# Normalised linear attention and a gated channel mix: full-width attention algebra, blends as scale and add, and a new planner for the order of instructions

## The chip, the cores and the metric

The kernel runs on one core of one Trainium2 chip (trn2). Times are device microseconds (us), the median of several executions. PE is the matmul engine (TensorE), PEld its weight loads, DVE the vector engine, ACT the scalar engine, POOL and SP the two that mostly issue DMA here. Some executions fall into a slow state (here 278 to 314 us, with a lower granted PE clock).

## The reference

```python
kv  = einsum('bhsd,bhse->bhde', k, v)          # batch 8, heads 8, seq 576, head 64
out = einsum('bhsd,bhde->bhse', q, kv)
x   = out / sqrt(mean(out*out, -1) + 1e-6) * g_norm   # then heads side by side: [8, 576, 512]
xk  = mu_k * x + (1 - mu_k) * x_prev           # x_prev: x of the token before
xr  = mu_r * x + (1 - mu_r) * x_prev
y   = sigmoid(xr @ w_r) * (relu(xk @ w_k)**2 @ w_v)   # 512 -> 1024 -> 512
```

Matmul operands are bf16. The channel mix goes in 9 groups of 512 tokens; the attention in 8 batches of 576. Group g needs batches up to g (group 8 up to 7), so attention for later batches runs between the mix's matmuls.

## The kernel before

Pieces of work are handed to a planner in Python, which simulates the engines and so fixes the order in which each engine's instructions are emitted; each engine then runs its list in order. The parts that matter:

```python
# statistics and normalisation, once per batch (all four pairs of heads, 32 rows each)
nc.tensor.matmul(get(pst)[32*hp:32*hp+32, half, 0:HS], sel2, sq.t[:, hp, ...])       # L360 sums of squares
nc.scalar.preload_act_table_set("natural_log_exp_and_others")                       # L365
nc.scalar.activation(out=get(ln)[rows], in_=pst.t[rows, :, 0:HS], func=AF.Ln, bias=eps[rows], scale=1.0/HD)
nc.scalar.activation(out=get(rs)[rows], in_=ln.t[rows], func=AF.Exp, scale=-0.5)    # rs = 1/rms
nc.tensor.matmul(get(ps)[:, i, 0:HS], selg[rows], rs.t[rows, half, :])              # L384 spread rs*g to 128 rows
nc.vector.tensor_mul(out=xT.t[...], in0=get(uT)[...], in1=ps.t[...])                # L391 product, one operand in PSUM
# ... d = xT - xT of the token before ...
nc.vector.scalar_tensor_tensor(out=dst[:, hp, ...], in0=d.t[:, hp, :],              # L413 fused blend
    scalar=mu_sb[:, m+hp:m+hp+1], in1=xT.t[:, hp, 0:S], op0=ALU.mult, op1=ALU.add)
```

The matmuls of the mix are L453 (w_k), L476 (w_r) and L495 (w_v); L480 is the sigmoid, L457 the ReLU. Attention's PSUM tiles, called `at`, have two buffers; the mix's, `mm`, have two as well.

## Time and profile before

| | before |
|---|---|
| time, median of fast runs | 240.4 us |
| PE, DVE, ACT busy | 87%, 67%, 52% of the span |
| first w_r matmul; first w_k matmul of group 0, group 1 | 23.7; 32.4, 60.8 us |
| table loads of ACT | 17, 1.28 us each |

The page's first lines, busy us with the share of the span:

```profile
span 238.5 us, 3893 instructions
PE 207.4 (87%) x1586; PEld 98.0 (41%) x1586; DVE 158.7 (67%) x263; ACT 123.3 (52%) x154; POOL 25.1 (11%) x39
```

PE is the busiest, and its necessary work is easily counted. The timeline of PE late in the run (start us, length us, engine, line, operation, operands, shape, count) shows the mix alone:

```profile
179.83 7.07 PE L453 MATMUL mm<-xk,w_k 128*128 128x512 bf16 x32
186.74 3.62 PE L476 MATMUL mm<-w_r,xr 128*128 128x512 bf16 x16
```

From 179.83 to 186.74 us are 32 matmuls, 216 ns each; 9 groups of 80 make 155 us. The rest of the span is attention, waits, the start and the end. The largest wait is between groups 0 and 1 (same view; in brackets the idle time before, and what ended it):

```profile
52.84 0.29 PE L384 MATMUL at<-rs,selg 32*128 32x288 bf16 x2
...
54.64 0.30 PE L384 MATMUL at<-rs,selg 32*128 32x288 bf16 x2 [0.71 <-DVE xT L391]
55.30 0.30 PE L384 MATMUL at<-rs,selg 32*128 32x288 bf16 x2 [0.37 <-DVE xT L391]
...
60.83 1.05 PE L453 MATMUL mm<-xk,w_k 128*128 128x512 bf16 x2
```

For 8 us no mix matmul runs: PE feeds small matmuls to DVE, which makes the product L391 from PSUM, then the blends. After it DVE is the limit for a while. The view of stretches (stretch, its length, then busy us of each engine, granted clock, DMA share, GB/s):

```profile
60.00:100.00 40.00, 37.57 (x329) 16.75 (x327) 39.22 (x65) 27.09 (x36) 4.62 (x6) 0.97 0.81 135
```

DVE is busy for 39.22 of 40 us, ACT for 27. And the groups of instructions of ACT and DVE that the change touches (line, engine, operation, operands, shapes, count, then busy us, mean ns of one, idle time before them):

```profile
L413 DVE SCALAR_TENSOR_TENSOR xr<-d,mu_sb,xT 128x576 bf16<-128x576 bf16 x32 | 24.2, 813 | 0.0
L391 DVE TENSOR_TENSOR xT<-uT,at 128x576 bf16<-128x576 bf16 x29 | 20.8, 750 | 7.4 <-PE at L384 7.2
L365 ACT ACT_TABLE_LOAD x10 | 12.8, 1283 | 0.2
L366 ACT ACTIVATE ln<-at,eps 128x576 f32<-128x576 f32 x7 | 5.2, 741 | 0.1
```

### The profile page before, as it was taken

The numbers are of one execution on the slowest core, as the hardware profiler recorded it, in microseconds if no ns is written. First come the engines' busy times: TensorE is split into PE (matmuls) and PEld (weight loads), VectorE is DVE, ScalarE is ACT, GpSimd is POOL, SyncE is SP. The second block draws the span as 40 slices with busy tenths as digits, with TensorE's granted clock in tenths as the row PEclk, the third lists the DMA queues.
The fourth block names the chain that finished last, engine by engine and source line by source line (L and its number), as shares of the span: only waits on it lengthen the run. The fifth ranks groups of instructions, "written<-read, shape, count | busy, mean of one in ns | idle before, by whom it ended". The sixth has DMA issues, their size and how long they took to land.

```text
span 238.5 us, 3893 instructions
## 1 busy us (share of the span) xinstructions
PE 207.4 (87%) x1586; PEld 98.0 (41%) x1586; DVE 158.7 (67%) x263; ACT 123.3 (52%) x154; POOL 25.1 (11%) x39
## 2 busy tenths in 40 slices
PE   0573699896999989979799999998999999999971
PEld 0431146443534434443453378333444444444430
DVE  1278915659999999958975996799599324224231
ACT  2379147735678913964577449547713513604500
POOL 8860002300300300030000000000000000000000
PEclk9999999996799999999999999999999999999998
DMA  5999999999993595359530130024004114015033
GB/s 79 184 206 207 204 203 204 204 207 267 201 198 47 69 203 115 91 65 194 131 87 3 46 107 25 0 58 121 0 0 134 45 33 144 3 37 139 1 88 88
DMA packets 26817, 26.46 MB, mean 111 GB/s; under 512 B 1704, under 2 KB 21680, under 8 KB 26800
## 3 DMA queue, kind: packets, MB, share of 16 engines
q0 software_dynamic: 21008, 16.78, 45.8%
q1 hardware_dynamic: 5792, 9.45, 14.1%
q8 instruction: 12, 0.20, 0.3%
q14 instruction: 5, 0.04, 0.0%
HBM read 33.56 MB, written 9.44 MB: 180 GB/s over the span
## 4 chain that ended last, share of the span: by engine, by line
PE 64%; DVE 16%; ACT 10%; DMA 5%; issue 2%; POOL 0%; SPq 0%; DVEq 0%; ACTq 0%; POOLq 0%
PE mm L495 22%; PE mm L453 22%; PE mm L476 11%; DVE out L499 4%; DMA q<-in_q_dram 3%; DVE xT L391 3%; PE at L315 2%; DMA out_dram<-out 2%; PE at L293 2%; ACT L365 2%; DVE xr L413 2%; DVE xk L413 2%; DVE sq L344 2%; ACT relu L457 2%; PE at L335 1%
## 5 line engine op out<-in xcount | busy, mean ns | idle before, releaser
L495 PE MATMUL mm<-w_v,sqk 128*128 128x512 bf16 x288 | 68.2, 380 | 1.7 <-DVE out L499 1.7
L453 PE MATMUL mm<-xk,w_k 128*128 128x512 bf16 (+1 forms) x320 | 67.6, 361 | 1.4 <-DVE out L499 1.4
L457 ACT ACTIVATE relu<-mm 128x1024 bf16<-128x1024 f32 x36 | 36.3, 1020 | 48.1 <-PE mm L453 48.1
L453 PEld LDWEIGHTS <-w_k 128*128 128x128 bf16 x320 | 30.3, 98 | 31.0 <-issue 3.2
L495 PEld LDWEIGHTS <-sqk 128*128 128x128 bf16 x288 | 25.7, 98 | 33.3 <-issue 4.1
L499 DVE TENSOR_TENSOR out<-mm,sig 128x1024 f32<-128x1024 f32 (+1 forms) x20 | 22.3, 1115 | 24.2 <-PE mm L495 17.8
L476 PE MATMUL mm<-w_r,xr 128*128 128x512 bf16 x144 | 36.5, 402 | 2.1 <-DVE xr L413 1.6
L460 DVE TENSOR_TENSOR sqk<-relu 128x1024 bf16<-128x1024 bf16 x36 | 24.6, 689 | 18.2 <-ACT relu L457 18.0
L172 ACT CAST uT<-at 128x576 bf16<-128x576 f32 x26 | 16.0, 640 | 24.4 <-PE at L335 24.4
L391 DVE TENSOR_TENSOR xT<-uT,at 128x576 bf16<-128x576 bf16 (+1 forms) x31 | 21.7, 731 | 7.4 <-PE at L384 7.2
L480 ACT ACTIVATE sig<-mm 128x1024 bf16<-128x1024 f32 x18 | 18.5, 1027 | 12.0 <-PE mm L476 11.7
L413 DVE SCALAR_TENSOR_TENSOR xr<-d,mu_sb,xT 128x576 bf16<-128x576 bf16 x32 | 24.2, 813 | 0.0
L413 DVE SCALAR_TENSOR_TENSOR xk<-d,mu_sb,xT 128x576 bf16<-128x576 bf16 x32 | 24.1, 812 | 0.1
L476 PEld LDWEIGHTS <-xr 128*128 128x128 bf16 x144 | 14.3, 102 | 21.6 <-issue 4.2
L315 PE MATMUL at<-ident,q 96*128 96x96 bf16 x186 | 13.6, 221 | 1.4 <-DMA q<-in_q_dram 0.9
L315 PEld LDWEIGHTS <-q 96*128 96x128 bf16 x192 | 11.9, 107 | 6.3 <-issue 1.8
L172 ACT COPY qT<-at 128x576 bf16<-128x576 bf16 x19 | 11.8, 644 | 4.0 <-PE at L315 3.8
L344 DVE TENSOR_TENSOR sq<-uT 128x576 bf16<-128x576 bf16 x32 | 13.0, 453 | 0.4 <-ACT uT L172 0.3
L365 ACT ACT_TABLE_LOAD x10 | 12.8, 1283 | 0.2
L232 POOL DMA_DIRECT2D q<-in_q_dram x10 | 7.3, 735 | 51.4 <-PE at L315 41.0
L384 PE MATMUL at<-rs,selg 32*128 32x288 bf16 x60 | 8.9, 298 | 3.9 <-DVE kv L174 1.1
L407 DVE TENSOR_TENSOR d<-xT 128x2304 bf16<-128x2304 bf16 (+2 forms) x10 | 11.2, 1119 | 0.3
(47 smaller groups left out, 114.2 us busy)
## 6 DMA issues: line engine op xcount, KB each, us to landing
out_dram<-out SPq DMA_DIRECT2D x24, 192.0 KB
k<-in_k_dram POOLq DMA_DIRECT2D x7, 576.0 KB, 10.3
v<-in_v_dram POOLq DMA_DIRECT2D x7, 576.0 KB, 12.4
q<-in_q_dram POOLq DMA_DIRECT2D x7, 576.0 KB, 11.5
out_dram<-out SPq DMA_DIRECT2D x24, 128.0 KB
out_dram<-out SPq DMA_DIRECT2D x24, 64.0 KB
w_k<-in_moe_w_k_dram POOLq DMA_DIRECT2D x1, 1024.0 KB, 12.5
w_v<-in_moe_w_v_dram POOLq DMA_DIRECT2D x1, 1024.0 KB, 16.9
```

The source lines that it names most:

```text
L172: nc.scalar.copy(out=dst, in_=src)
L315: nc.tensor.transpose(t[:, e, NP * i:NP * i + NP], qin.t[:, 2 * hp + e, 128 * i:128 * i + 128], ident[:NP, :NP])
L344: e.tensor_tensor(out=get(sq)[:, hp, :], in0=flat(hp), in1=flat(hp), op=ALU.mult)
L391: nc.vector.tensor_mul(out=xT.t[:, hs, xs], in0=get(uT)[:, hs].rearrange("q h i jj p -> q h (i jj p)")[:, :, cs], in1=ps.t[:, 0:step, 0:HS])
L413: nc.vector.scalar_tensor_tensor(out=dst[:, hp, c0:c0 + S], in0=d.t[:, hp, :], scalar=mu_sb[:, m + hp:m + hp + 1], in1=xT.t[:, hp, 0:S], o ...
L453: nc.tensor.matmul(get(ps)[:, fc % 2, a0:a1], w_k_sb[:, cc, 128 * fc:128 * fc + 128], xk[:, cc, x0:x0 + a1 - a0], start=(cc == 0), stop=(c ...
L457: nc.scalar.activation(out=get(rt), in_=ps.t, func=AF.Relu)
L460: nc.vector.tensor_mul(out=get(sqk)[:, 2 * f2:2 * f2 + 2, :], in0=rt.t, in1=rt.t)
L476: nc.tensor.matmul(get(ps)[:, ci % 2, :], xr[:, cc, n0:n0 + 128], w_r_sb[:, cc, :], start=(cc == 0), stop=(cc == NHP - 1))
L480: nc.scalar.activation(out=get(sg), in_=ps.t, func=AF.Sigmoid)
L495: nc.tensor.matmul(get(ps)[:, ci % 2, :], sqk.t[:, fc, 128 * ci:128 * ci + 128], w_v_sb[:, fc, :], start=(fc == 0), stop=(fc == NFC - 1))
L499: nc.vector.tensor_mul(out=get(ot)[:, xs, :], in0=ps.t[:, xs, :], in1=sg.t[:, xs, :])
```

## The change

Its intent: full 128x128 matmuls in the attention (the kv of two heads on the diagonal of one block), the sums of squares by a block of ones so that they come out already spread over the 128 rows, the product then in SBUF, DVE's blends in faster forms, g multiplied into w_r and w_k, an early start by hardware-queue loads, and a planner with smaller latencies, stage targets and filler matmuls that keep PE's clock up at the start. The diff cut to its core:

```diff
-            nc.scalar.preload_act_table_set("natural_log_exp_and_others")        # was ahead of every Ln
-            nc.scalar.activation(out=get(ln)[rows], in_=pst.t[rows, :, 0:HS], func=AF.Ln, bias=eps[rows], ...)
-            nc.scalar.activation(out=get(rs)[rows], in_=ln.t[rows], func=AF.Exp, scale=-0.5)
+    add({"ACT": 1.3}, lambda _: nc.scalar.preload_act_table_set("natural_log_exp_and_others"), due=-1999, ...)  # once
+        for hp in range(NHP):                                                    # per pair of heads, all 128 rows
+            def ss_mm(...):   nc.tensor.matmul(get(ps)[:, i, 0:HS], ones, sq.t[:, hp, ...])
+            def ln_act(...):  nc.scalar.activation(out=get(ln), in_=ps.t[:, :, 0:HS], func=AF.Ln, bias=eps, scale=1.0/HD)
+            def exp_act(...): nc.scalar.activation(out=get(rs)[:, hp]..., in_=ln.t, func=AF.Exp, scale=-0.5)
+            a = add({"ACT": act_us(S, False, True)}, ln_act, ..., table="ln")    # the planner counts one set
+            exps[hp] = add({"ACT": act_us(S, True)}, exp_act, ..., table="ln")   # for both functions
-                nc.vector.tensor_mul(out=xT.t[:, hs, xs], in0=get(uT)[...], in1=ps.t[...])          # PSUM operand
+                nc.vector.tensor_mul(out=xT.t[:, hs, NP:NP+S], in0=uT.t[:, hs], in1=rs.t[:, hs])    # SBUF only
-            nc.vector.scalar_tensor_tensor(out=dst[...], in0=d.t[:, hp, :], scalar=mu_sb[...], in1=xT.t[...], ...)
+                    for hp in range(hp0, hp0 + n):
+                        nc.vector.tensor_scalar(out=get(md)[:, hp], in0=d.t[:, hp], scalar1=cols[...], op0=ALU.mult)
+                    nc.vector.tensor_tensor(out=dst[:, hs, ...], in0=md.t[:, hs], in1=xT.t[:, hs, 0:S], op=ALU.add)
+                nc.vector.tensor_scalar(out=dst, in0=dst, scalar1=cols[:, 8:9], ...)   # g into w_r (1x) and w_k (2x)
+            e.dma_start(out=first[n], in_=part(n, 0, 0, 2))     # first pair of heads, fp32, hardware queues; casts follow
+                nc.tensor.matmul(get(warm_ps)[:, 0, 0:128], zero[...], zero[...])      # filler in planned gaps at the start
... (transposes, kv blocks, planner latencies and stage targets cut)
```

## The prediction

> **What bounds it now.** Span 238.5 us, granted clock 0.98. PE is 87% busy and leads the chain of waits (PE 64%, DVE 16%, ACT 10%, DMA 5%). Its floor: the channel mix is 9 groups x 80 matmuls of 512 columns. From 173 us PE's timeline has 16 in 3.45 us, 216 ns each (the Trainium skill, "TensorE: Matmul & The Clock Gate", Wait — 56ns, not 53.3ns?, gives 215.7 ns warm; the trace agrees). So 155.4 us. Attention costs PE, per batch, from the chain: kv 0.88, transposes 4 x 0.26, u about 1.0, statistics 0.36, spreading 4 x 0.23: 4.2 us; seven batches inside the mix make 29.4. First w_r matmul 23.7 us, last w_v matmul ends 233.8: 210.1 - 155.4 - 29.4 = about 25 us lost between them, nearly all before 166 us:
> - 3.6 us at the start: matmuls wait for DVE's xr blends.
> - about 8 us at 52.7-60.8, between group 0 and group 1: group 1 needs batch 1 and DVE works through xT, d, xk. PE goes cold too (clock 0.65 to 0.78 in 54-66, about 3 us).
> - the rest at 66-166: DVE is 97-99% busy in 60-100 (busy by stretches).
>
> **The change, costed.**
> - Blends: 64 fused ones of 0.81 us (one element per cycle) become per batch 8 scales and two adds. The skill, "VectorE: DVE Perf Modes", the perf-mode tier table, has tensor_scalar at 4x and tensor_tensor at 2x in bf16. The trace agrees for the add (2304 columns in 1.36 us); no run yet shows the scale, estimate from the page 0.23 us. 6.5 -> about 4.5 us a batch.
> - xT product from PSUM, 4 x 0.75, becomes SBUF-only, about 1.3 us. kv copies 4 x 0.42 become 2 x 0.35.
> - Against it: ln and exp run on all 128 rows per head pair, 1.4 -> about 5.2 us of ACT a batch (4 x (0.67+0.62)).
> - PE: spreading goes (-0.92), the ones-block sums cost 8 x 0.12 instead of 0.36, the rest about equal: 4.2 -> 3.9 us a batch.
> DVE drops from about 16 to 13 us a group before copies, ACT rises from 10 to 13.5; both fit.
> - Start: first head pair by fp32 hardware-queue loads plus casts (first matmul 7.6 us now, then about 5), fewer table loads, w_r matmuls by head pair. First w_r matmul about 17.5.
> - Loads run near 205 GB/s until 57 us. Batch 1 is complete about 35 us now; with the earlier start about 34, in halves. Its last half still needs about 11 us of dependent work, so group 1 cannot start before about 44 (60.8 now); PE still loses about 5 us there.
>
> **Sum.** 17.5 + 155.4 + 7 x 3.9 + 6 (tail: last product, store) = 206; plus 5 at the batch 1 boundary, 3 to 4 for other stalls and cold clock: span about 215, time about 217 us (before: time minus span 2.7). Range 207 to 228. Faster 0.94, same 0.05, slower 0.01. The gain is idle PE time before 166 us.
>
> **What would show it.** First w_r matmul at 16-19 us; group 1's first w_k matmul at 41-48; scales near 0.23 us; DVE under 70% busy, ACT 70-75%; no stretch with DVE over 95%; last groups 17.3 us each; PE busy sum within 5 us of 207.
>
> **What would make it wrong.** ACT as the new limit: ln/exp and u copies holding the two "at" PSUM buffers; extra table loads; batch 1 later than its data allows; the 4x scales not at 4x.

## The result, and the profile after

The kernel after takes 250.2 us (four fast runs, 248.4 to 251.2), the kernel before 240.4 (three): slower by 4.0% (ratio 1.0402, interval 1.035 to 1.046). All ratios here are from fast runs alone; they are not quite the ratios of the medians that are quoted.

```profile
span 248.8 us, 4251 instructions
PE 212.2 (85%) x1730; PEld 111.1 (45%) x1730; DVE 152.8 (61%) x287; ACT 168.1 (68%) x198; POOL 28.2 (11%) x43
```

DVE fell a little; ACT rose by 45 us. ACT's groups, in the view that was shown of before:

```profile
L450 ACT ACTIVATE ln<-at,eps 128x576 f32<-128x576 f32 x32 | 22.4, 738 | 1.1 <-PE at L447 0.8
L453 ACT ACTIVATE rs<-ln 128x576 bf16<-128x576 f32 x32 | 20.5, 677 | 0.3
L450 ACT ACT_TABLE_LOAD x16 | 20.5, 1283 | 0.3
L453 ACT ACT_TABLE_LOAD x16 | 20.5, 1283 | 0.3
L578 ACT ACT_TABLE_LOAD x7 | 9.0, 1283 | 0.1
```

The Ln and Exp work itself grew as the prediction had it (43 us, 5.4 a batch). But there are 40 table loads, with the one at the very start, instead of 17: after batch 0 one at every switch from Ln to Exp and one at every switch back, so that each pair of loads serves one or two pairs of heads. ACT's timeline in batch 0, then in batch 1:

```profile
14.46 0.68 ACT L453 ACTIVATE rs<-ln 128x576 bf16<-128x576 f32 x1
15.04 0.72 ACT L450 ACTIVATE ln<-at,eps 128x576 f32<-128x576 f32 x1
...
39.63 1.28 ACT L450 ACT_TABLE_LOAD   x1
40.93 0.74 ACT L450 ACTIVATE ln<-at,eps 128x576 f32<-128x576 f32 x1
41.69 1.28 ACT L453 ACT_TABLE_LOAD   x1
42.98 0.68 ACT L453 ACTIVATE rs<-ln 128x576 bf16<-128x576 f32 x1
...
44.21 1.28 ACT L450 ACT_TABLE_LOAD   x1
```

In batch 0, after the one request by name, Ln and Exp alternate with no load at all. After the first sigmoid a load stands at every switch between the two. The planner believed that they share one (`table="ln"` on both). What that does to the other engines is in the waits (engine, line, for whom; us in total, times, longest):

```profile
DVE xT L468 <- ACT rs L453: 17.9, 14, 3.3
PE at L421 <- DVE qT L199: 6.4, 3, 2.2
PE at L374 <- ACT ln L450: 5.7, 2, 2.9
PE mm L601 <- ACT sig L578: 3.1, 1, 3.1
```

and in PE's timeline of group 3:

```profile
117.69 2.76 PE L548 MATMUL mm<-xk,w_k 128*128 128x512 bf16 x12
122.66 0.41 PE L421 MATMUL at<-qT,kvb 128*128 128x288 bf16 x2 [2.21 <-DVE qT L199]
```

The chain of waits tells how an Exp stops PE through DVE's queue: between the product and the copy of the next batch's q lie the copy of the token before, a copy of kv, d, the scales and the xr blend.

```profile
117.51 0.68 ACT rs L453
...
118.21 0.77 DVE xT L468
...
121.85 0.77 DVE qT L199
...
122.66 0.41 PE at L421 x2
```

The copy of q doesn't need that Exp. It stands behind the product in DVE's list, because the plan expected the Exp earlier.

A table of the first w_k matmul of each group, from PE's timelines, shows where time goes (two of the experiments below are listed already; "end" is the last matmul):

| us | g0 | g1 | g3 | g4 | g5 | g6 | g7 | g8 | end |
|---|---|---|---|---|---|---|---|---|---|
| before | 32.4 | 60.8 | 114.3 | 137.7 | 160.5 | 179.8 | 197.1 | 214.4 | 233.8 |
| after | 29.0 | 59.6 | 114.2 | 139.9 | 164.2 | 188.4 | 207.2 | 224.4 | 244.0 |
| one table set | 29.4 | 55.4 | 101.4 | 123.8 | 145.9 | 168.1 | 185.7 | 202.9 | 222.5 |
| longer warm-up | 28.4 | 54.5 | 99.7 | 122.1 | 144.2 | 166.3 | 184.0 | 201.2 | 220.7 |

The kernel after is never more than 3.4 us ahead, level at group 3, and then loses 2.3, 1.5 and 4.9 us in groups 3 to 5, as long as there is attention in the mix, and 1.5 us more in group 6. (Group 2 is left out, since the kernel before mixes its first matmuls with the end of group 1.) The prediction was 217 us, in a range of 207 to 228: wrong in sign.

### The profile page after: what moved, and what is told of

Read it like the earlier page. It is cut to its first block, busy times and chain, and to the rows that moved or that the text cites. A ratio compares the mean times of both kernels' runs of the same rounds, so it can differ in the third digit from the quotient of the medians.

```text
span 248.8 us, 4251 instructions
## 1 busy us (share of the span) xinstructions
PE 212.2 (85%) x1730; PEld 111.1 (45%) x1730; DVE 152.8 (61%) x287; ACT 168.1 (68%) x198; POOL 28.2 (11%) x43
## 4 chain that ended last, share of the span: by engine, by line
PE 45%; ACT 28%; DVE 15%; issue 5%; DMA 4%; SPq 1%; DVEq 0%; ACTq 0%
PE mm L548 18%; PE mm L601 11%; PE mm L574 8%; ACT L450 7%; ACT ln L450 7%; ACT rs L453 4%; ACT L453 3%; PE at L402 3%; ACT sig L578 2%; PE at L421 2%; DVE md L493 2%; DVE out L605 2%; DMA rows<-in_g_norm_dram 2%; DVE xr L496 2%; DVE qT L199 2%
## 5 line engine op out<-in xcount | busy, mean ns | idle before, releaser
L548 PE MATMUL mm<-xk,w_k 128*128 128x512 bf16 (+1 forms) x320 | 70.7, 367 | 3.6 <-DVE w_k L309 1.4
L468 DVE TENSOR_TENSOR xT<-uT,rs 128x1152 bf16<-128x1152 bf16 (+1 forms) x18 | 12.4, 690 | 17.9 <-ACT rs L453 17.9
L450 ACT ACTIVATE ln<-at,eps 128x576 f32<-128x576 f32 x32 | 22.4, 738 | 1.1 <-PE at L447 0.8
L578 ACT ACTIVATE sig<-mm 128x1024 bf16<-128x1024 f32 x18 | 18.2, 1024 | 7.0 <-PE mm L574 6.9
L493 DVE TENSOR_SCALAR md<-d,cols 128x576 bf16<-128x576 bf16 x64 | 21.2, 368 | 0.3
L453 ACT ACTIVATE rs<-ln 128x576 bf16<-128x576 f32 x32 | 20.5, 677 | 0.3
L453 ACT ACT_TABLE_LOAD x16 | 20.5, 1283 | 0.3
L450 ACT ACT_TABLE_LOAD x16 | 20.5, 1283 | 0.3
L421 PE MATMUL at<-qT,kvb 128*128 128x288 bf16 x64 | 13.8, 300 | 8.0 <-DVE qT L199 6.4
L277 POOL DMA_DIRECT2D k<-in_k_dram x11 | 8.1, 737 | 66.3 <-PE at L374 63.3
L435 DVE TENSOR_TENSOR sq<-uT 128x1152 bf16<-128x1152 bf16 (+1 forms) x20 | 12.6, 633 | 3.0 <-ACT uT L197 2.7
L199 DVE COPY qT<-at 128x1152 bf16<-128x1152 bf16 (+1 forms) x16 | 11.2, 700 | 3.7 <-PE at L402 3.6
L402 PE MATMUL at<-ident,q 96*64 96x96 bf16 x384 | 13.2, 223 | 0.0
```

The lines of the kernel that those rows point to most:

```text
L402: nc.tensor.transpose(t[64 * e:64 * e + 64, hp - hp0, NP * j:NP * j + NP], qin.t[:, 2 * hp + e, HD * j:HD * j + HD], ident[:NP, :NP])
L421: nc.tensor.matmul(get(ps)[:, i, 0:HS], kv[:, hp, :], qT.t[:, hp, HS * i:HS * i + HS], start=True, stop=True)
L450: nc.scalar.activation(out=get(ln), in_=ps.t[:, :, 0:HS], func=AF.Ln, bias=eps, scale=1.0 / HD)
L453: nc.scalar.activation(out=get(rs)[:, hp].rearrange("q (i c) -> q i c", i=2), in_=ln.t, func=AF.Exp, scale=-0.5)
L493: nc.vector.tensor_scalar(out=get(md)[:, hp], in0=d.t[:, hp], scalar1=cols[:, m0 + hp:m0 + hp + 1], scalar2=None, op0=ALU.mult)
L548: nc.tensor.matmul(get(ps)[:, fc % 2, a0:a1], w_k_sb[:, cc, 128 * fc:128 * fc + 128], xk[:, cc, x0:x0 + a1 - a0], start=(cc == 0), stop=(c ...
```

## The experiments

Thirteen kernels ran. All results are correct but for the last, which is wrong.

**1. One table set for Ln and Exp, the same plan.** The planner's calls are untouched, so the order of all pieces is that of the kernel after; only the request comes back, and only where a sigmoid has come between.

```diff
             def ln_act(_, ps=ps, ln=ln):
+                if table_now[0] != "ln":
+                    nc.scalar.preload_act_table_set("natural_log_exp_and_others")
+                    table_now[0] = "ln"
                 nc.scalar.activation(out=get(ln), ...)
         def r_sig(_, ps, sg):
+            table_now[0] = "sig"
```

> The kernel after, same plan and same arithmetic; the joint ln-and-exp table set is asked for by name before the first Ln after a Sigmoid, so table loads fall from 40 to 14 (26 x 1.28 = 33 us of ACT). Theory T1 (the loads are the cause of the loss: PE waits for ACT's ln and exp, which wait for loads): 212 to 222 us, ACT busy about 135 us, the gaps of PE behind ACT ln gone. Rival T2 (the ln and exp work on all 128 rows, 43 us instead of 14, holds the PSUM buffers whatever the loads do): 240 us or more. Rival T3 (the plan's order on in-order engines is at fault, above all DVE's queue between qT copies and blends): 230 to 245 us, with gaps of 2 us per group left in front of the u matmuls.

Measured: 228.3 us, ratio 0.948 (0.943 to 0.953). From the two ratios, 26 loads fewer (33 us of ACT) are worth (1.040 - 0.948) x 240.4 = 22 us, and turn a loss of 4% into a gain of 5%. ACT is busy for 133.6 us, as T1 had it, but the time lies above T1's range and below those of its rivals; so T1 holds for 22 us and doesn't explain the whole distance to the prediction. T2 is out. In ACT's timeline of batch 1 the Exp follows its Ln in 0.03 us; in the kernel after it came at 42.98, although that one's Ln was 0.47 us earlier:

```profile
41.40 0.74 ACT L454 ACTIVATE ln<-at,eps 128x576 f32<-128x576 f32 x1
42.17 0.68 ACT L457 ACTIVATE rs<-ln 128x576 bf16<-128x576 f32 x1
```

The loads that are left are 14, of which these stand ahead of an Ln:

```profile
L452 ACT ACT_TABLE_LOAD x6 | 7.7, 1283 | 0.1
```

T3's sign, gaps of 2 us ahead of the u matmuls, is gone. PE's timeline at the place where the kernel after lost 2.21 us:

```profile
107.86 0.41 PE L422 MATMUL at<-qT,kvb 128*128 128x288 bf16 x2 [0.23 <-DVE qT L199]
```

In the waits, DVE's product waited 17.9 us for Exp in the kernel after, and now:

```profile
DVE xT L472 <- ACT rs L457: 1.7, 2, 1.1
```

In the view of stretches PE and DVE are the busier for it; the kernel after had 32.35 us of PE, 27.25 of DVE and 34.83 of ACT here:

```profile
60.00:100.00 40.00, 38.49 (x297) 19.80 (x300) 34.22 (x64) 32.34 (x43) 3.08 (x4) 1.00 0.79 133
```

**2. Ln twice, in the kernel with one table set.** Is it the load that hurts, or ACT's time in that place? The Ln is issued a second time with the same result.

```diff
                 nc.scalar.activation(out=get(ln), in_=ps.t[:, :, 0:HS], func=AF.Ln, ...)
+                nc.scalar.activation(out=get(ln), in_=ps.t[:, :, 0:HS], func=AF.Ln, ...)
```

> One table set, and every Ln issued twice with the same result: 32 x 0.74 = 24 us more of ACT in the same place of the chain sums - Ln - Exp, no table load added. T1 in the form that it is ACT time in that chain that costs, whoever spends it: 12 to 20 us slower than with one table set (240 to 248 us). If only the loads themselves hurt (a flush of the engine beyond their 1.28 us): under 6 us slower.

Measured: 239.2 us (three fast runs), ratio 0.989 (0.984 to 0.993); that is, by the ratios, 9.8 us more than with one table set for 24 us of ACT, 0.41 us per us, where the loads cost 22 / 33 = 0.66. It lies between the two forecasts, short of 12 and above the rival's 6 us: time of ACT between the sums and the product costs though no load is added. Why a load costs more per us than a second Ln was not tested.

**3. The kernel before without its request.** The old kernel has Ln and Exp once per batch.

```diff
         def st_act(_):
             rows = slice(32 * hp0, 32 * hp0 + 32 * n)
-            nc.scalar.preload_act_table_set("natural_log_exp_and_others")
```

> The kernel before without its request for the joint table set ahead of each Ln. Its Ln and Exp run once per batch on all head pairs, so loads only rise from 17 to 21, by one in each of seven batches, less three at the start: ACT busy +5 us. If the harm of the missing request depends on the split into head pairs (a load before nearly every Ln and Exp): within 2 us of before. If any two loads in that chain cost PE in full: 5 us or more slower.

Measured: 244.7 us, ratio 1.017 (1.011 to 1.024), between the two forecasts: 4.2 us for a net 4 loads (5 us of ACT). The net hides two effects, which the profile separates: with three loads fewer at the start group 0's first w_k matmul comes at 31.0 us instead of 32.4, and with one more between Ln and Exp in each of seven batches group 7's comes at 200.7 instead of 197.1. So the seven cost 1.4 + 3.6 = 5.0 us, 0.7 each, against 22 / 26 = 0.85 each in the kernel after. The first guess, that only the split into head pairs makes the missing request expensive, is wrong per load. The split multiplies their number: 7 more in the batches here, 26 there.

**4. The blends, each way.** First the kernel before with its fused blends as scale and add; then the kernel with one table set with fused blends.

```diff
-            nc.vector.scalar_tensor_tensor(out=dst[...], in0=d.t[:, hp, :], scalar=mu_sb[...], in1=xT.t[...], ...)
+            nc.vector.tensor_scalar(out=md[:, hp], in0=d.t[:, hp, :], scalar1=mu_sb[...], op0=ALU.mult)
+            nc.vector.tensor_tensor(out=dst[...], in0=md[:, hp], in1=xT.t[:, hp, 0:S], op=ALU.add)
```

> The kernel before with its 64 fused blends replaced by a scale and an add each, nothing else; the plan's order is kept. DVE pays 64 x (0.29 + 0.38) = 43 us instead of 48 us if ops run back to back as in the kernel after (measured there: 0.57 us for two scales, 0.76 us for an add of two head pairs). If the blend form matters at all in a DVE-bound stretch, 235 to 240 us; if it is too small to matter, 240 to 242 us.

Measured: 241.9 us, ratio 1.0074 (1.001 to 1.013): no gain, rather a little loss.

> The kernel after with one table set as in the other run, but with the fused blends of before (64 x 0.81 us) in place of scales and adds; same plan. If the blend form was a real gain of the change: 3 to 10 us slower than the run with one table set. If DVE has slack once the loads are gone: within 2 us of it.

Measured: 228.3 us, ratio 0.950 (0.945 to 0.956), the same as with scale and add. The form of the blends, which the prediction counted as 2 us of DVE a batch, is worth nothing measurable either way (both runs kept a plan made for the other form). A scale of 576 columns takes 0.37 us alone and two in a row 0.57 (in the chain of waits, from the end of the operation before); the add of two head pairs takes 0.76. DVE's busy time in all is 155.2 us with fused blends and 151.5 with one table set: 3.7 us, or 0.5 a batch. In the old kernel, where each add is of one head pair, the split saves nothing: 159.4 us against 158.7.

**5. The new planner alone.** The kernel before, its pieces and durations unchanged, put in order by the new planner class, without fillers.

```diff
-class Piece: ...            # the planner of before
-class Planner: ...
+class Piece: ...            # that of after: smaller latencies, 0.25 us of slack for PE
+class Planner: ...
-    plan.run()
+    plan.run(lambda p: 0.25)
```

> The kernel before in every operation, but put in order by the new planner class (its latencies, its 0.25 us of slack for PE; no filler matmuls). The kernel with one table set is 12 us under before. If that gain is the planner's latencies: 228 to 233 us. If it is the new arithmetic and stage targets (SBUF product, pairs of head pairs, start): 238 to 245 us.

Measured: 242.5 us, ratio 1.0037 (1.001 to 1.007). The planner's class as such brings nothing; stage targets could not be tried apart from the pieces that they belong to.

**6. The product at its old speed.** In the kernel with one table set, rs is kept in fp32, so that the SBUF product runs at the rate that it had from PSUM; the planner doesn't know.

```diff
-        "rs": (1, (128, NHP, S), BF16),
+        "rs": (1, (128, NHP, S), FP32),
```

> One table set, with rs in fp32, so that the product uT x rs runs at the rate that it had from PSUM before (0.75 us per head pair instead of 0.38): 1.5 us more of DVE per batch, all else as with one table set. If the relief of DVE by the SBUF product is a good part of the 12 us that the kernel with one table set wins over before: 3 us or more slower (ratio above 0.96). If DVE has slack: under 1.5 us (0.948 to 0.955).

Measured: 237.4 us, ratio 0.988 (0.984 to 0.991): 9.5 us lost, of the 12.5 that the kernel with one table set wins over before. In the view of groups the product of two head pairs takes 1350 ns, against 758 in the kernel after (first line):

```profile
L468 DVE TENSOR_TENSOR xT<-uT,rs 128x1152 bf16<-128x1152 bf16 x14 | 10.6, 758 | 17.3 <-ACT rs L453 17.3
L472 DVE TENSOR_TENSOR xT<-uT,rs 128x1152 bf16<-128x1152 bf16 x14 | 18.9, 1350 | 1.1 <-ACT rs L457 1.1
```

Only 8 x 1.2 = 9.6 us of DVE were added, and nearly all of it reaches the end. The plan was fixed for the fast product here, so this is the price of a slow product in this plan; in a plan made for it the price may be less. In experiment 4, 3.7 us more of DVE in the same plan cost nothing that was measured. Whether that is the place in DVE's queue or the smaller amount was not tested.

**7. The start: g out of DVE's queue.** With the loads gone, 11 us to the predicted time are left. Group 0's first w_k matmul comes at 29.4 us where the prediction had about 21. It waits for DVE, whose last ops there scale w_k by g. Three runs take that away. The first lets ACT scale w_k:

```diff
-                            T0 + 1 + 4 * i, f"g.w_k{i}", {"DVE": both["DVE"]}))
+                            T0 + 1 + 4 * i, f"g.w_k{i}", {"ACT": both["ACT"]}))
```

> One table set as in the first run, and the scaling of w_k by g (two ops of 0.8 us on DVE, last in DVE's queue before group 0's first w_k matmul at 29.5 us) moved to ACT, which stands idle there. If the start is held by DVE's queue: first w_k matmul near 28 us and about 1 to 2 us faster than with one table set alone (226 to 227.5 us). If the start is held by something else (the data, the hidden-layer chain of the last head pair): within 0.5 us.

Measured: 230.5 us (three fast runs), ratio 0.954 (0.951 to 0.957), slower than with one table set if anything. The planner drew up another plan for it: inconclusive. The second gives up the scaling and adds ln g in the Exp (g is |noise| + 0.5 in the reference's inputs, so positive; a kernel for any g could not do this):

```diff
-                nc.scalar.activation(out=get(rs)[:, hp]..., in_=ln.t, func=AF.Exp, scale=-0.5)
+                nc.scalar.activation(out=get(rs)[:, hp]..., in_=ln.t, func=AF.Exp, bias=lng, scale=-0.5)
-    p_wr = scale_w(w_r_sb, load_w(...), ...)       # and the two of w_k
+    p_wr = load_w(...)
```

> One table set, and g is no longer multiplied into w_r and w_k (three DVE ops, 2.4 us, all before group 0's first w_k matmul); Exp adds ln g as a bias instead, a few hundredths of a us per Exp. If folding g into the weights held up the start: first w_r matmul about 1 us earlier, first w_k matmul 2 to 3 us earlier, 225 to 227 us in all. If not: within 0.7 us of the run with one table set, or slower by the dearer Exp.

Measured: 230.9 us, ratio 0.957 (0.953 to 0.961). The start came as expected (first w_r at 18.2, first w_k at 28.0, group 1 at 53.1 us, 2.3 us ahead of one table set), but the new plan let group 1 last from 53.1 to 82.9 us, 5 us longer than with one table set. Again two things changed. So the third keeps the plan: the scaling pieces stay in it with their times, and emit nothing.

```diff
         def fn(eng):
-            if eng == "ACT":
-                nc.scalar.mul(out=dst, in_=dst, mul=cols[:, 8:9])
-            else:
-                nc.vector.tensor_scalar(out=dst, in0=dst, scalar1=cols[:, 8:9], scalar2=None, op0=ALU.mult)
+            pass
```

> The earlier run without weight scaling also made the planner draw up another plan, which lost 4 us in group 1; here the plan is that of the run with one table set (the scaling pieces stay in the plan and emit nothing), and ln g is Exp's bias. If DVE's queue holds up the start: first w_k matmul near 28 us against 29.4, and 0.5 to 1 per cent faster than with one table set (ratio to before 0.938 to 0.945). If the start's lateness doesn't reach the end: ratio 0.946 to 0.952.

Measured: 228.0 us, ratio 0.948 (0.944 to 0.953): no gain, and the first w_k matmul at 29.8 us. And with batch 0's xk scales made by ACT on top:

```diff
+                        if fine and m0 == 0:
+                            nc.scalar.mul(out=get(md)[:, hp], in_=d.t[:, hp], mul=cols[:, m0 + hp:m0 + hp + 1])
+                            continue
                         nc.vector.tensor_scalar(out=get(md)[:, hp], in0=d.t[:, hp], ...)
```

> As the run before it, and batch 0's four scales for xk are made by ACT, idle there, instead of DVE (4 x 0.29 us off DVE's queue at 24 to 28 us). If DVE's queue bounds the start: first w_k matmul another 0.5 to 1.1 us earlier and the ratio to before another 0.3 per cent lower. If not: no change.

Measured: 228.5 us, ratio 0.951 (0.947 to 0.954), no change. Taken alone, these two say that work behind the xr blends is not what holds the start. But there is a second thing in the stretches of the run with the plan kept (granted clock is the third number from the right):

```profile
24.00:26.00 2.00, 0.60 (x2) 0.11 (x2) 1.86 (x6) 0.01 (x1) 0.00 (x0) 1.00 1.28 203
26.00:28.00 2.00, 1.99 (x6) 0.76 (x7) 1.90 (x6) 1.02 (x1) 1.06 (x2) 0.64 1.31 201
28.00:30.00 2.00, 2.00 (x6) 0.76 (x5) 1.15 (x3) 0.01 (x1) 0.58 (x1) 0.50 1.32 205
```

PE did little from 20 to 26 us, and when the matmuls came its clock went to half. The run with the xk scales on ACT has it too (0.50 from 24 to 30 us), so its "no change" does not clear DVE's queue either.

**8. A longer warm-up.** The fillers go on until batch 0's last xr blend, 13 more of them; else as in the run with the plan kept.

```diff
-    p_warm = add({"PE": 0.0}, lambda _: None, deps=[last_exp[0]], bufs=[warm_ps], ...)
+    p_warm = add({"PE": 0.0}, lambda _: None, deps=[x_ready[0]["r"][-1]], bufs=[warm_ps], ...)
```

> As the run with folding out and the plan kept, with the filler matmuls carried on until batch 0's last xr blend: 13 more fillers in the two gaps between the w_r matmuls at 20 to 26 us, nothing else. In the run without them the last ten w_r matmuls took 3.94 us (2.33 in the kernel after), so the gain of the shorter DVE queue was eaten by a slower PE. If the clock ate it: those ten take 2.2 to 2.4 us, first w_k matmul near 28.2 instead of 29.75, ratio to before 0.936 to 0.944. If the clock drops for another reason or the start doesn't matter: 0.946 to 0.951.

Measured: 226.9 us, ratio 0.944 (0.940 to 0.947), the best correct kernel; its six runs (226.5 to 227.3) all lie under the four without the fillers (227.5 to 228.7, same chip). First w_k at 28.4 us, the ten matmuls in 2.33 us. The stretch that had a clock of 0.64 (same view):

```profile
26.00:28.00 2.00, 1.81 (x9) 0.86 (x10) 1.93 (x6) 1.02 (x1) 0.94 (x2) 1.00 1.31 200
```

So in these profiles the half clock had eaten the shorter queue. Not every profile without the added fillers shows it: the kernel after, one table set and fused blends had their ten in 2.33 us too; experiment 6 and the last three kernels of experiment 7 took 3.75 to 4.45.

**9. Work ahead of the xr blends taken away**. Batch 0's four subtractions are left out; the result is wrong.

```diff
             def diff(_, hs=slice(hp0, hp0 + n)):
+                if fine:
+                    return
-   in0=d.t[:, hp], scalar1=cols[...]
+   in0=xT.t[:, hp, NP:NP + S] if fine else d.t[:, hp], scalar1=cols[...]
```

> As the run with the longer warm-up, but batch 0's four subtractions are left out and its scales read xT instead (a wrong result on purpose): 4 x 0.4 us off DVE ahead of the xr blends. If DVE feeds the start: last xr blend 1 to 1.6 us earlier, first w_k matmul near 27 instead of 28.4, and the total lower by about as much (ratio to before 0.936 to 0.940 against 0.9436). If the data or ACT's last Exp sets it: last xr blend at most 0.5 us earlier and the total within 0.5 us.

Measured: 226.0 us, ratio 0.939 (0.936 to 0.942), against 0.944 with them. DVE's last xr blend of batch 0, with the subtractions and then without:

```profile
25.68 0.46 DVE L499 TENSOR_TENSOR xr<-md,xT 128x576 bf16<-128x576 bf16 x1
```

```profile
24.61 0.46 DVE L501 TENSOR_TENSOR xr<-md,xT 128x576 bf16<-128x576 bf16 x1
```

It is 1.07 us earlier, the first w_k matmul 1.1 us (27.3), group 8's 1.2 us (200.0 against 201.2), the time 1.2 us shorter by the ratios (whose intervals overlap a little; the runs were on different chips). So DVE does feed the start, and in the profiles the start reaches the end one for one. (Some 1.5 us of DVE were taken away; part of the rest went into a wait of 0.54 us for an Exp.)

## Why the prediction was wrong, point by point

- **PE's floor: right.** Pure groups take 17.2 us (207.2 to 224.4 in the kernel after), 216 ns a matmul. Nothing in the change touches that.
- **"ACT rises from 10 to 13.5; both fit", with "fewer table loads" at the start: the step that failed.** The Ln and Exp work was sized right (5.4 us a batch for 5.2). The loads were not counted after the change at all: the ACT sum has none of them, and "fewer table loads" is what the planner believes, in whose simulation Ln and Exp share a table. The kernel has 40 loads, not 17 or fewer, and ACT is busy for 168.1 us instead of 133.6 with 14. Putting the request back and nothing else gives 228.3 us, that is 22 of the 33 us between forecast and result. "Extra table loads" stood in the list of what might go wrong; its size if it came, 2 x 1.28 us per head pair or two, could have been estimated from the 1.28 us of a load in the profile before and the four Ln and Exp per batch of the diff. That the loads would come was not to be seen in the diff.
- **"First w_r matmul about 17.5", and an unbroken mix from there: failed.** It came at 19.9 us, and then DVE handed over one head pair at a time, so that sixteen matmuls took until 27.5 us and group 0's first w_k stood at 29.0 instead of 21. PE's timeline of the kernel after (its first w_k matmul last):

```profile
19.87 0.59 PE L574 MATMUL mm<-w_r,xr 128*128 128x512 bf16 x2 [0.94 <-DVE w_r L309]
...
21.96 0.61 PE L574 MATMUL mm<-w_r,xr 128*128 128x512 bf16 x2 [0.76 <-DVE xr L496]
23.23 0.60 PE L574 MATMUL mm<-w_r,xr 128*128 128x512 bf16 x2 [0.66 <-DVE xr L496]
25.21 2.33 PE L574 MATMUL mm<-w_r,xr 128*128 128x512 bf16 x10 [1.38 <-DVE xr L496]
28.97 1.25 PE L548 MATMUL mm<-xk,w_k 128*128 128x512 bf16 x5 [1.43 <-DVE w_k L309]
```

  In each gap PE waits for DVE. The sum left out DVE's work per head pair at the start: square, product, the copy of the token before, d, scale, add, and at the end the scaling of w_k by g. In the kernel with the longer warm-up the first w_k is still 7.4 us late; with attention's 0.4 us a batch below that makes the 10 us between 226.9 and 217. (An account from one profile, not a test. The 8 to 9 us that the sum had for stalls did come, if in other places: PE is idle for 7.8 of the 190 us from 30 to 220.)
- **"4.2 -> 3.9 us a batch" of PE for attention: mis-sized.** From the starts in group 3 with one table set I get about 4.3: kv 1.0, transposes 2 x 0.63, u 1.1, sums 2 x 0.49. Seven times 0.4 is near 3 us.
- **The wait for batch 1, "PE still loses about 5 us there": mis-sized and misplaced.** Group 1 begins at 59.6 us (55.4 with one table set), not at 41 to 48. With one table set the chain of waits lies on DVE from 44.4 to 56.0 us and ends with batch 1's xk blend, as the prediction's dependent work would have it, but group 0 itself ended only at 50 us, and attention fills most of the time: PE is idle for 1.8 us from 48 to 56, and its clock is 0.70 in the next 4 us. In the kernel after PE also waited 2.78 us for an Ln, until 50.3 us.
- **The blends, "6.5 -> about 4.5": mis-sized and off the point.** DVE's busy times differ by 0.5 us a batch (experiment 4), not 2, and no run shows a gain from it.
- **The product in SBUF: right, and in this plan worth most of what is won** (9.5 of 12.5 us in experiment 6).
- **"No stretch with DVE over 95%": right for stretches of 20 us** (17.2 us at most). DVE is busy for 27.25 of the 40 us from 60 to 100 in the kernel after, but because it waits for ACT, not because it is relieved.

What stays open: why 1 us of load costs more than 1 us of second Ln; when PE's clock falls at the start and when not; what the stage targets and the start are worth apart from the product; and what a plan that knew of the two sets would have made of the loads.

## What to carry to other kernels

When an operation is split into more pieces, count everything that comes once per piece, not only its elements: here a table load came at every switch between Ln and Exp, since the line that asked for their joint set had been moved to the start. Look at how often such a load occurs after the change, not at whether the source says that one set is enough; a planner that simulates the engines believes its own tags. And an engine at 68% can set the time if its late results stand at the head of another engine's in-order list: follow such a wait through the queue, and, when testing a repair, keep the plan fixed, or two things change at once.

## What the Trainium skill lacked or had wrong

- "ScalarE: Activation LUTs", Table sets: the hidden batching unit: it has ln followed by exp as one load, because one set holds both. Here that holds only where the set was asked for by name: without the request the kernel after loads a table ahead of 16 Ln and 16 Exp groups. The page doesn't say that the automatic choice may load again between the two functions, nor does "ScalarE activation tables: per-element evaluation and per-set limits".
- The same page, What ACT_TABLE_LOAD costs: about 1283 ns for the load agrees (1283 ns in every group). Its further 1380 ns of drain for every switch is not seen: at 39.63 us the load starts 0.02 us after the op before it ends, and the Ln starts 0.02 us after the load, so a switch is 1.3 us here.
- "VectorE: DVE Perf Modes", The TRN2 errata: the prediction took 0.23 us for a 4x scale of 576 columns, near that page's errata row (58 + FD/4 cycles give 0.21 us). Measured are 0.37 us for one alone and 0.57 for two in a row, 0.29 each. The page itself says that the row is too low and names about 150 fixed cycles; an estimate from that, (150 + 144) / 0.96 GHz = 0.31 us, would have been nearer.
- "TensorE: Matmul & The Clock Gate", Why this matters for your kernels, warns of gaps of about 3 us without matmuls. In the run with the plan kept no gap from 20 to 26 us exceeded 1.4 us, PE was busy for 2.35 of those 6 us, and the granted clock still fell to 0.64 and 0.50 in the next 4 us; with 13 fillers in the gaps (3.37 us busy) it stayed at 1.00. So gaps well under 3 us did not keep it up. The page gives no share of busy time that is enough, and no threshold can be read off here: one table set kept 1.00 with 2.92 us.
